# A fused RWKV-6 and max-out MLP kernel: the first units' decay sums in fp32, weight preparation on other engines, and a new order of the list

## The chip, the core and the metric

The kernel runs on one core of a Trainium2 chip. The core has five engines with a queue of instructions each: TensorE (PE, matmuls; its weight loads are shown apart as PEld), VectorE (DVE), ScalarE (ACT), GpSimd (POOL) and SyncE (SP), which here issues all transfers between the chip's memory and the core's. An engine works its queue strictly in order and waits on semaphores where an operand is not there yet. The metric is device microseconds (us) of one execution, the median of several runs. The kernel before takes 164.98 us (five runs, 164.53 to 165.4).

## The reference

Inputs are `r, k, v, w` of 4 sequences x 8 heads x 768 steps x 48, a vector `u` per head, and the weights of a small MLP. The first half is a linear attention with a decay per step and channel; the second a max-out MLP on the 3072 rows that result:

```python
for t in range(S):
    cur = einsum('bhd,bhe->bhde', u[None] * kt, vt)
    y[:, :, t] = einsum('bhd,bhde->bhe', rt, state + cur)
    state = wt[:, :, :, None] * state + einsum('bhd,bhe->bhde', kt, vt)
...
h1 = x @ w1; h2 = x @ w2
g = maximum(h1, h2)
return g @ w_out
```

## The kernel before, in words

**Tiling.** The 768 steps are cut into 6 chunks of 128, and the 4 sequences into 2 pairs. A chunk of one pair is a *unit*; there are 12, numbered 0 to 11, worked in the order chunk 0 pair 0, chunk 0 pair 1, chunk 1 pair 0 and so on. The 128 steps lie on the 128 partitions. Within a unit many steps are made per sequence (`.0` and `.1`).

**The stages of a unit.** `ldw, ldk, ldr, ldv` (L226) load 384 KB each, in pieces of 192 bytes in memory. `lw` (L232, ACT) takes the logarithm of the decay `w`. The running sum of these logarithms over the chunk is a matmul with a triangular matrix, `ex` (L241 to L245). So that it can run on TensorE's reduced fp32 format, the logarithm is split into a high part `lwh` (L236, ACT, a second logarithm written in that format) and a rest `lwl` (L239, DVE), and `ex` is two matmuls that add up in PSUM. From the sum come `incl` (L250, DVE), `aex` and `ainv` (L255, L258, ACT exponentials), and with them the scaled `rp` (L278) and `kp` (L281, both DVE). `T` (L311, PE) transposes these, `TO` (L318, ACT) copies them out of PSUM, `M` (L327, PE) makes the scores, `MO` (L332, DVE) masks them, and `Y` (L343, L347, PE) multiplies by the values `vb` (L304, ACT) and the state. The step's own term is made by `ku` (L288, POOL), `rku` (L292, DVE), `dg` (L297, DVE) and `bv` (L301, POOL), and `YO` (L354, DVE) adds it. `K, sa, sm, sb` carry the state (`sb`, L396, on POOL); `row`, `wt`, `wx` take the chunk's last decay sum through memory (L262, L267) to the layout of the state.

**The MLP.** `X` (L361, PE) and `XO` (L365, ACT) transpose the unit's 256 result rows. The maximum is written as (h1+h2)/2 + |h1-h2|/2. So `H` (L406, PE, four steps a unit, 12 matmuls each group of two) multiplies by the weight difference `wd_sb`, `HO` (L412, ACT) takes half the absolute value, `O1` and `O2` (L416 and L422, PE) multiply by `w_out`, and the linear half goes in one matmul by `wc_sb` = (w1+w2) w_out / 2. `OO` (L431, ACT) copies the result out, `st` (L437, SP) stores it.

**Weight preparation, once.** `ldw12.0` to `.2` load three blocks of w1 and w2 (1 MB each, two transfers), `ldwo.0` and `.1` two halves of `w_out` (768 KB each). These five share two buffers (tag `w12`, L178 and L184), so a block's load waits until the one two places earlier has been used. `wsum` (L196, POOL) and `wdif` (L199, DVE) make sum and difference in bf16; `wT` (L204, PE) transposes the sum into a PSUM tile of tag `mlp`, of which there are two, shared with `H`, `wp`, `O1` and O2; `wTO` (L208, DVE) copies it out; `woc` (L190, POOL) casts `w_out`; `wp` (L213, PE) and `wpO` (L218, ACT) make `wc_sb`. `warm` (L173) are matmuls on a blank tile that keep TensorE busy while there is nothing else.

**What sets the order.** Nothing is scheduled by the compiler. `ORDER` (L17 to L66) is a list written out by hand, one word a step; the steps are issued in that order, each to its engine's queue. So the list fixes the order of every queue, SP's included, and the order in which transfers are asked for. A transfer also waits for the one eight places before it in SP's queue.

Of the kernel before, what the change touches and what calls it, by code (L numbers as in the profile page):

```python
# [26 lines left out]
M.1.0 TO.1.1 H.0.1 MO.1.0 wt.0 ex.3.0 woc.1 HO.0.0 HO.0.1 dg.1.1 H.0.2 ldw.4 incl.3.0 ldv.1.1 M.1.1 HO.0.2
kp.2 wp.0 aex.3.0 rp.2 ex.3.1 row.2 wpO.0 H.0.3 sa.0 bv.1.0 vb.1.0 ldv.2 MO.1.1 aex.3.1 Y.1.0 ldk.3 T.2.0 ku.2
wx.0 HO.0.3 wp.1 TO.2.0 YO.1.0 incl.3.1 lwh.4 wp.2 sm.0 rku.2 lw.4 wpO.1 T.2.1 lwl.4 row.3 vb.1.1 M.2.0 ldw.5
wpO.2 K.1 dg.2 bv.1.1 ldr.3 TO.2.1 Y.1.1 ex.4.0 sb.0.0 O1.0.0 sa.1 vb.2 MO.2.0 sb.0.1 wt.1 aex.4.0 O2.0.0 bv.2  # L30
ainv.3 incl.4.0 K.2 YO.1.1 M.2.1 ex.4.1 sa.2 ku.3 ldr.4 Y.2.0 MO.2.1 aex.4.1 ldk.4 X.1.0 X.1.1 OO.0.0 O1.0.1
XO.1 YO.2.0 lw.5 incl.4.1 O2.0.1 wt.2 kp.3 H.1.0 OO.0.1 lwh.5 X.2.0 rp.3 Y.2.1 H.1.1 HO.1.0 lwl.5 ldw.6 wx.1
T.3.0 HO.1.1 row.4 H.1.2 YO.2.1 TO.3.0 rku.3 H.1.3 ainv.4 ex.5.0 sm.1 X.2.1 ldv.3 HO.1.2 M.3.0 rp.4 T.3.1
ldw.7 XO.2 O1.1.0 MO.3.0 ku.4 HO.1.3 TO.3.1 O2.1.0 ldv.4 dg.3 aex.5.0 H.2.0 OO.1.0 kp.4 M.3.1 wx.2 HO.2.0
H.2.1 incl.5.0 ldk.5 H.2.2 rku.4 HO.2.1 ex.5.1 lw.6 sm.2 O1.1.1 vb.3 sb.1.0 incl.5.1 wt.3 dg.4 HO.2.2 sb.1.1
O2.1.1 lwh.6 bv.3 K.3 MO.3.1 T.4.0 OO.1.1 H.2.3 st.0.0 TO.4.0 lwl.6 st.0.1 O1.2.0 HO.2.3 row.5 sa.3 sb.2.0
vb.4 M.4.0 Y.3.0 sb.2.1 ldr.5 lw.7 MO.4.0 T.4.1 wt.4 bv.4 O2.2.0 aex.5.1 ainv.5 YO.3.0 ex.6.0 K.4 lwh.7
incl.6.0 ku.5 Y.3.1 st.1.0 sa.4 O1.2.1 OO.2.0 ldk.6 YO.3.1 aex.6.0 ldw.8 wx.3 TO.4.1 X.3.0 kp.5 ex.6.1 X.3.1
O2.2.1 XO.3 lwl.7 M.4.1 OO.2.1 st.1.1 Y.4.0 rp.5 aex.6.1 H.3.0 H.3.1 incl.6.1 HO.3.0 sm.3 T.5.0 ainv.6 ldr.6
YO.4.0 H.3.2 HO.3.1 rku.5 ex.7.0 ldv.5 HO.3.2 H.3.3 sb.3.0 MO.4.1 TO.5.0 O1.3.0 ku.6 HO.3.3 dg.5 ldk.7 aex.7.0  # L40
X.4.0 T.5.1 lw.8 incl.7.0 Y.4.1 sb.3.1 TO.5.1 M.5.0 YO.4.1 O2.3.0 MO.5.0 row.6 ex.7.1 OO.3.0 X.4.1 O1.3.1 XO.4
incl.7.1 kp.6 lwh.8 O2.3.1 ldv.6 rp.6 st.2.0 M.5.1 OO.3.1 H.4.0 wx.4 bv.5 MO.5.1 T.6.0 HO.4.0 H.4.1 vb.5 wt.5
H.4.2 lwl.8 aex.7.1 ldw.9 HO.4.1 Y.5.0 ldr.7 K.5 HO.4.2 YO.5.0 ex.8.0 ainv.7 sa.5 H.4.3 rku.6 TO.6.0 Y.5.1
st.2.1 O1.4.0 YO.5.1 vb.6 kp.7 HO.4.3 X.5.0 X.5.1 T.6.1 sm.4 XO.5 wt.6 O2.4.0 dg.6 sb.4.0 aex.8.0 M.6.0 TO.6.1
st.3.0 sb.4.1 H.5.0 incl.8.0 ldw.10 MO.6.0 K.6 bv.6 OO.4.0 ex.8.1 row.7 wx.5 lw.9 H.5.1 incl.8.1 HO.5.0 M.6.1
sm.5 Y.6.0 HO.5.1 rp.7 H.5.2 ainv.8 O1.4.1 sb.5.0 sa.6 lwh.9 row.8 YO.6.0 ku.7 ldv.7 HO.5.2 MO.6.1 T.7.0
st.3.1 X.6.0 O2.4.1 TO.7.0 ldk.8 H.5.3 lwl.9 aex.8.1 ldr.8 T.7.1 OO.4.1 rku.7 lwh.10 Y.6.1 O1.5.0 lw.10 sb.5.1
dg.7 ldk.9 HO.5.3 ex.9.0 YO.6.1 M.7.0 vb.7 bv.7 incl.9.0 O2.5.0 TO.7.1 MO.7.0 O1.5.1 ldv.8 OO.5.0 lwl.10
aex.9.0 X.6.1 O2.5.1 XO.6 ku.8 Y.7.0 OO.5.1 ex.9.1 st.4.0 YO.7.0 wx.6 H.6.0 incl.9.1 H.6.1 HO.6.0 kp.8 M.7.1
HO.6.1 K.7 st.4.1 rp.8 ainv.9 H.6.2 row.9 H.6.3 MO.7.1 aex.9.1 HO.6.2 T.8.0 ldr.9 HO.6.3 st.5.0 O1.6.0 sa.7  # L50
TO.8.0 sm.6 ku.9 ex.10.0 M.8.0 incl.10.0 ldw.11 Y.7.1 T.8.1 aex.10.0 YO.7.1 wt.7 O2.6.0 sb.6.0 vb.8 MO.8.0
X.7.0 sb.6.1 X.7.1 OO.6.0 O1.6.1 XO.7 kp.9 ldv.9 TO.8.1 O2.6.1 rku.8 ldr.10 K.8 OO.6.1 H.7.0 rku.9 H.7.1
HO.7.0 dg.8 st.5.1 M.8.1 HO.7.1 H.7.2 rp.9 ex.10.1 HO.7.2 bv.8 H.7.3 incl.10.1 ldk.10 Y.8.0 MO.8.1 HO.7.3
T.9.0 wt.8 lw.11 O1.7.0 YO.8.0 wx.7 lwh.11 sm.7 Y.8.1 sa.8 TO.9.0 O1.7.1 sb.7.0 ldk.11 YO.8.1 wt.9 sb.7.1 dg.9
ainv.10 X.8.0 X.8.1 O2.7.0 aex.10.1 lwl.11 XO.8 T.9.1 rp.10 ldv.10 M.9.0 OO.7.0 O2.7.1 ldr.11 vb.9 bv.9 MO.9.0
H.8.0 OO.7.1 ex.11.0 HO.8.0 H.8.1 incl.11.0 TO.9.1 st.6.0 Y.9.0 kp.10 H.8.2 aex.11.0 ku.10 YO.9.0 HO.8.1 M.9.1
ex.11.1 HO.8.2 MO.9.1 st.6.1 T.10.0 wx.8 H.8.3 TO.10.0 ldv.11 incl.11.1 K.9 rku.10 O1.8.0 st.7.0 aex.11.1
HO.8.3 sm.8 ainv.11 T.10.1 sa.9 M.10.0 wx.9 TO.10.1 kp.11 Y.9.1 st.7.1 X.9.0 O2.8.0 vb.10 sb.8.0 YO.9.1 O1.8.1
MO.10.0 sb.8.1 X.9.1 rp.11 O2.8.1 XO.9 M.10.1 dg.10 OO.8.0 Y.10.0 OO.8.1 T.11.0 sm.9 H.9.0 TO.11.0 MO.10.1
bv.10 H.9.1 HO.9.0 st.8.0 T.11.1 HO.9.1 st.8.1 H.9.2 sb.9.0 YO.10.0 M.11.0 sb.9.1 HO.9.2 H.9.3 MO.11.0 ku.11  # L60
Y.10.1 HO.9.3 O1.9.0 TO.11.1 YO.10.1 X.10.0 X.10.1 rku.11 O2.9.0 XO.10 O1.9.1 dg.11 OO.9.0 vb.11 M.11.1 bv.11
O2.9.1 MO.11.1 H.10.0 OO.9.1 st.9.0 Y.11.0 HO.10.0 H.10.1 YO.11.0 H.10.2 HO.10.1 st.9.1 Y.11.1 HO.10.2 X.11.0
# [7 lines left out]
def kernel(  # L70
# [19 lines left out]
    FO = d_ff // C  # L90
# [17 lines left out]
    triU = const.tile([C, C], F32)  # L108
    make_upper_triangular(nc, triU, val=1.0, diag=False)
    triR = const.tile([C, C], F32R)  # L110
# [8 lines left out]
    for i in range(2):  # L119
        eng = nc.vector if i == 0 else nc.gpsimd  # L120
        rp = const.tile([C, NB, H, DP], BF16, name=f"rp{i}")
        kp = const.tile([C, NB, H, DP], BF16, name=f"kp{i}")
# [18 lines left out]
    ws_sb = const.tile([C, KO, d_ff], BF16)  # L141
    wo_sb = const.tile([C, FO, HD], BF16)
    wsT_sb = const.tile([C, FO, HD], BF16)
# [3 lines left out]
    st = {}  # L147
# [4 lines left out]
    def flat(x):  # L152
        return x.rearrange("p h d -> p (h d)")
# [14 lines left out]
    def warm(tag):  # L168

        def fn(count):  # L170
            x = ps.tile([C, 512], F32, tag=tag, bufs=2 if tag == "mlp" else 1, name="warm")
            for _ in range(count):
                nc.tensor.matmul(x, ident, blank)  # L173
        return fn
# [12 lines left out]
        st["wof", half] = x  # L187

    def woc(half):
        nc.gpsimd.tensor_copy(wo_sb[:, half * FO // 2:(half + 1) * FO // 2, :], st["wof", half])  # L190

    def ldu():
        nc.sync.dma_start(out=u_b, in_=u.rearrange("h d -> (h d)").unsqueeze(0).to_broadcast([C, HD]))

    def wsum(ko):
        nc.gpsimd.tensor_add(ws_sb[:, ko, :], st["w12", ko][:, 0, :], st["w12", ko][:, 1, :])  # L196

    def wdif(ko):
        nc.vector.tensor_sub(wd_sb[:, ko, :], st["w12", ko][:, 0, :], st["w12", ko][:, 1, :])  # L199
# [5 lines left out]
        st["wT", ko] = tp  # L205

    def wTO(ko):
        nc.vector.tensor_copy(wsT_sb[:, :, ko * C:(ko + 1) * C], st.pop(("wT", ko)))  # L208

    def wp(ko):  # L210
        wc_p = ps.tile([C, HD], F32, tag="mlp", bufs=2)
# [28 lines left out]

    def ex(i, b):  # L241
        ex_p = ps.tile([C, HD], F32, tag="ex", name="ex_p")
        nc.tensor.matmul(ex_p, triR, flat(st["lwh", i][:, b]), start=True, stop=False)  # L243
        nc.tensor.matmul(ex_p, triR, flat(st["lwl", i][:, b]), start=False, stop=True)  # L244
        st["ex", i, b] = ex_p  # L245

    def incl(i, b):
# [186 lines left out]
    def out_st(i, b):  # L434
# [5 lines left out]
               ldw=ld("w", w), ldk=ld("k", k), ldr=ld("r", r), ldv=ld("v", v),  # L440
               lw=lw, lwh=lwh, lwl=lwl, ex=ex, incl=incl, aex=aex, ainv=ainv, row=row, wt=wt, wx=wx, rp=rp, kp=kp,
               ku=ku, rku=rku, dg=dg, bv=bv, vb=vb, T=T, TO=TO, M=M, MO=MO, Y=Y, YO=YO, X=X, XO=XO,
               K=K, sa=sa, sm=sm, sb=sb, H=Hf, HO=HO, O1=O1, O2=O2, OO=OO, st=out_st, **{f"warm_{t}": warm(t) for t in ('kv',)})
    with tc.manual_schedule():
        for step in ORDER.split():
            name, *at = step.split(".")
# [38 lines left out]
```

## Time and profile before

| | us |
|---|---|
| median of 5 runs (lowest, highest) | 164.98 (164.53, 165.4) |
| the profiled execution, whole | 164.53 |
| its span in the profile | 162.8 |
| busy: PE, DVE, ACT, POOL | 148.8, 133.7, 118.4, 75.9 |
| of PE's, the warm matmuls (68 recorded) | 19.1 |
| first matmul of `H.0.0`; of `O1.0.0` | 33.58; 47.42 |
| DVE's last instruction ends | 148.9 |
| PE's last matmul ends; last `OO` starts | 159.4; 159.50 |

The page of a profile cuts the span in 40 slices and gives each engine's busy share in tenths. The windows view gives the busy time in chosen stretches. The timeline lists instructions with start and length, and, in brackets, how long the engine had stood idle and what released it. The groups view sums instructions of one line. Lengths overlap a little: consecutive DVE instructions listed with 0.55 us start 0.47 apart.

### The profile page before, as it was taken

To read this page: it belongs to the slowest core of one execution; us is meant where nothing else is said; L and a number is where in the kernel's file an instruction comes from. 1 tells how busy PE (TensorE), PEld (TensorE's weight loads), DVE (VectorE), ACT (ScalarE), POOL (GpSimd) and SP (SyncE) were. 2 spreads that over 40 slices of the span, in tenths; PEclk is the share of its full clock that TensorE was granted. 3 is DMA by queue.
4 is the path that set the end of the run, shared out by engine and by line. 5 is a ranking of instruction groups with operands and counts; after the bars stand their busy time and mean duration, and the time that the engine had idled before them with its cause. 6 is when DMAs were issued, how large, how long until landed. Compare 5 with 4: busy or idle time off the path is not lost.

```text
span 162.8 us, 3999 instructions
## 1 busy us (share of the span) xinstructions
PE 148.8 (91%) x1604; PEld 101.9 (63%) x1606; DVE 133.7 (82%) x171; ACT 118.4 (73%) x202; POOL 75.9 (47%) x68
## 2 busy tenths in 40 slices
PE   6997798659979999999899999999999999999991
PEld 2444444447656865768668678677777677767760
DVE  3296999899979999999998999999989999762000
ACT  5153743775797997898969998987789796765641
POOL 8284597451685085832530375932158343730000
PEclk9999999999999999999999999999999999999999
DMA  5989998998999899599999829978899932011202
GB/s 101 322 171 259 377 220 174 268 299 139 207 227 155 153 229 224 131 197 212 234 187 207 187 59 261 212 209 164 189 171 206 229 109 76 25 52 48 79 17 97
DMA packets 112758, 28.82 MB, mean 177 GB/s; under 512 B 107738, under 2 KB 111962, under 8 KB 112740
## 3 DMA queue, kind: packets, MB, share of 16 engines
q1 hardware_dynamic: 112740, 28.58, 80.7%
q8 instruction: 12, 0.20, 0.5%
q14 instruction: 6, 0.05, 0.1%
HBM read 23.82 MB, written 4.75 MB: 176 GB/s over the span
## 4 chain that ended last, share of the span: by engine, by line
PE 48%; DVE 22%; SPq 12%; DMA 7%; issue 6%; ACT 3%; DVEq 0%; ACTq 0%
PE o_p L416 15%; PE g_p L406 12%; SPq L226 9%; PE o_p L422 6%; DVE MTm L332 5%; DMA rt<-in_r_dram 3%; PE tp L311 3%; DMA wt<-in_w_dram 3%; PE mt_p L327 3%; PE y_p L343 3%; DVE ku L292 3%; DVE dg L297 2%; DVE xs L354 2%; PE ex_p L243 2%; DVE rp L278 2%
## 5 line engine op out<-in xcount | busy, mean ns | idle before, releaser
L406 PE MATMUL g_p<-xT,wd_sb 128*128 128x256 bf16 x288 | 37.8, 273 | 2.0 <-ACT xT L365 1.4
L416 PE MATMUL o_p<-wo_sb,gT 128*128 128x384 bf16 x192 | 37.5, 326 | 0.0
L412 ACT ACTIVATE gT<-g_p 128x512 bf16<-128x512 f32 x48 | 28.2, 599 | 8.0 <-PE g_p L406 7.4
L301 POOL TENSOR_TENSOR bv<-vt,dg 128x768 f32<-128x768 f32 (+1 forms) x14 | 21.0, 1500 | 22.1 <-issue 8.1
L406 PEld LDWEIGHTS <-wd_sb 128*128 128x128 bf16 x288 | 26.3, 98 | 7.7 <-issue 3.2
L332 DVE TENSOR_TENSOR MTm<-mt_p,triU 128x1024 bf16<-128x1024 f32 x24 | 29.1, 1211 | 2.1 <-PE mt_p L327 2.1
L288 POOL TENSOR_TENSOR ku<-kt,u_b 128x768 f32<-128x768 f32 (+1 forms) x14 | 24.6, 1758 | 9.4 <-DMA kt<-in_k_dram 7.6
L318 ACT COPY rkT<-tp 128x1024 bf16<-128x1024 bf16 x24 | 24.4, 1017 | 5.0 <-PE tp L311 5.0
L396 POOL CAST sz<-sf 48x384 bf16<-48x384 f32 x20 | 14.1, 703 | 27.7 <-DVE sf L389 17.5
L416 PEld LDWEIGHTS <-gT 128*128 128x128 bf16 x192 | 18.0, 98 | 11.0
L173 PE MATMUL warm<-blank,ident 128*128 128x512 bf16 x68 | 19.1, 425 | 1.6 <-POOL ident masks.py:199 1.5
L255 ACT ACTIVATE Aex<-ex_p 128x384 f32<-128x384 f32 x24 | 11.9, 497 | 10.3 <-PE ex_p L244 6.5
L239 DVE TENSOR_TENSOR lwl<-lw,lwh 128x768 fp32r<-128x768 f32 (+1 forms) x14 | 15.9, 1144 | 3.2 <-ACT lwh L236 2.0
L292 DVE TENSOR_TENSOR ku<-rt,ku 128x768 f32<-128x768 f32 (+1 forms) x14 | 16.7, 1195 | 1.2 <-POOL ku L288 1.2
L431 ACT COPY osb<-o_p 128x384 f32<-128x384 f32 x24 | 11.6, 487 | 7.2 <-PE o_p L416 6.3
L278 DVE TENSOR_TENSOR rp<-rt,Aex 128x768 bf16<-128x768 f32 (+1 forms) x14 | 14.6, 1039 | 2.3 <-ACT Aex L255 2.3
L354 DVE TENSOR_TENSOR xs<-y_p,bv 128x384 bf16<-128x384 f32 x24 | 13.2, 548 | 3.1 <-PE y_p L347 2.4
L422 PE MATMUL o_p<-wc_sb,xT 128*128 128x384 bf16 x72 | 15.7, 326 | 0.0
L250 DVE TENSOR_TENSOR incl<-ex_p,lw 128x384 f32<-128x384 f32 x24 | 13.1, 548 | 1.2 <-PE ex_p L244 0.9
L232 ACT ACTIVATE lw<-wt 128x768 f32<-128x768 f32 (+1 forms) x14 | 10.5, 753 | 4.6 <-DMA wt<-in_w_dram 3.2
L173 PEld LDWEIGHTS <-ident 128*128 128x128 bf16 x70 | 6.9, 107 | 9.8 <-issue 3.2
L281 DVE TENSOR_TENSOR kp<-kt,Ainv 128x768 bf16<-128x768 f32 (+1 forms) x14 | 12.3, 881 | 0.1
(54 smaller groups left out, 231.4 us busy)
## 6 DMA issues: line engine op xcount, KB each, us to landing
out_dram<-osb SPq DMA_DIRECT2D x24, 192.0 KB, 2.0
wt<-in_w_dram SPq DMA_DIRECT2D x10, 384.0 KB, 4.4
kt<-in_k_dram SPq DMA_DIRECT2D x10, 384.0 KB, 5.7
rt<-in_r_dram SPq DMA_DIRECT2D x10, 384.0 KB, 7.3
vt<-in_v_dram SPq DMA_DIRECT2D x10, 384.0 KB, 4.3
w<-in_moe_w_dram SPq DMA_DIRECT2D x6, 512.0 KB, 5.4
wof<-in_moe_w_out_dram SPq DMA_DIRECT2D x2, 768.0 KB
wt<-in_w_dram SPq DMA_DIRECT2D x4, 192.0 KB, 5.7
```

Of the source, the lines that this page charges most:

```text
L173: nc.tensor.matmul(x, ident, blank)
L278: nc.vector.tensor_mul(rps[i % 2][:, seqs(b), :, 0:D], get("r", i, b), get("Aex", i, b))
L288: nc.gpsimd.tensor_mul(rows_(x), rows_(get("k", i, b)), u_b.unsqueeze(1).to_broadcast([C, x.shape[1], HD]))
L292: nc.vector.tensor_mul(rows_(get("ku", i, b)), rows_(get("r", i, b)), rows_(get("ku", i, b)))
L301: nc.gpsimd.tensor_mul(x, get("v", i, b), get("dg", i, b).unsqueeze(3).to_broadcast(list(x.shape)))
L318: nc.scalar.copy(rkT, st.pop(("tp", i, b)))
L332: nc.vector.tensor_mul(x.rearrange("p a q c -> p (a q) c"), st.pop(("mt", i, b)).rearrange("p a q c -> p (a q) c"), triU.unsqueeze(1).to_b ...
L354: nc.vector.tensor_add(x, st.pop(("y", i, b)), flat(st["bv", i][:, b]))
L406: nc.tensor.matmul(g_p[:, q, :], wd_sb[:, ko, fo * C:(fo + 1) * C], st["xT", i][:, ko].rearrange("p b c -> p (b c)"), start=(ko == 0), sto ...
L412: nc.scalar.activation(st["gT", i][:, f2 * 2:f2 * 2 + 2, :], st.pop(("g", i, f2)), AF.Abs, scale=0.5)
L416: nc.tensor.matmul(st["o", i, b], st["gT", i][:, fo, b * C:(b + 1) * C], wo_sb[:, fo, :], start=False, stop=(fo == FO - 1))
L422: nc.tensor.matmul(st["o", i, b], st["xT", i][:, ko, b, :], wc_sb[:, ko, :], start=(ko == 0), stop=False)
```

## The change

It has five parts.

1. `ex` looks whether the unit has a low part. If not, it is one matmul in full fp32 of the logarithm itself with the fp32 triangle. Units 0, 1 and 2 have no `lwh` and `lwl` any more (five of each in the list: two halves of unit 0, two of unit 1, unit 2 whole). The other units are as before.
2. `wsum` moves from POOL to DVE.
3. `wTO` moves from DVE to ACT.
4. `woc` moves from POOL to ACT.
5. The list is reordered from its first word to its last. It holds 57 warm matmuls where it held 70, some of them in other PSUM tiles (`warm_mt`, `warm_y`). Loads: k0.0 is second where r0.0 was; the second weight block comes after unit 0's loads and half of unit 1's; the third block comes after unit 0's values, unit 2's decay and the first half of `w_out`, where it had been before all of these.

```diff
 ORDER (beginning; loads up to the third weight block)
-ldw.0.0 ldr.0.0 ldw12.0 ldw.0.1 lw.0.0 ldk.0.0 lwh.0.0 lwl.0.0 ldw.1.0 warm_kv.10 ex.0.0 aex.0.0 ldw.1.1
-rp.0.0 ldu wdif.0 ldk.0.1 lw.0.1 incl.0.0 wsum.0 ldr.0.1 lwh.0.1 ainv.0.0 ldw12.1 lw.1.0 lwh.1.0 lwl.0.1
-ldw12.2 lwl.1.0 warm_kv.22 ex.0.1 ku.0.0 wT.0 incl.0.1 ku.0.1 aex.0.1 ldv.0.0 ainv.0.1 warm_kv.3 ex.1.0 lw.1.1
+ldw.0.0 ldk.0.0 ldw12.0 ldu lw.0.0 ldw.0.1 warm_kv.8 ex.0.0 ldr.0.0 incl.0.0 ldk.0.1 ldr.0.1 ldw.1.0 ku.0.0
+ldr.1.0 wsum.0 lw.0.1 ainv.0.0 aex.0.0 ldw12.1 kp.0.0 warm_kv.13 ex.0.1 rp.0.0 ldk.1.0 wT.0 incl.0.1 T.0.0
+wdif.0 ainv.0.1 aex.0.1 wTO.0 ku.0.1 ldw.1.1 TO.0.0 rku.0.0 ldv.0.0 lw.1.0 warm_kv.12 ex.1.0 ldv.0.1 incl.1.0
+ldw.2 rku.0.1 aex.1.0 wdif.1 ldwo.0 wsum.1 lw.1.1 ainv.1.0 rp.0.1 row.0 warm_kv.14 wT.1 kp.0.1 M.0.0 rp.1.0
+ex.1.1 kp.1.0 T.0.1 ldw12.2 aex.1.1 MO.0.0 TO.0.1 ldw.3 incl.1.1 lw.2 warm_kv.4 M.0.1 dg.0.0 T.1.0 vb.0.0
+dg.0.1 bv.0.0 ex.2.0 vb.0.1 MO.0.1 TO.1.0 bv.0.1 Y.0.0 YO.0.0 woc.0 ku.1.0 warm_kv.3 Y.0.1 X.0.0 YO.0.1
+aex.2.0 ldwo.1 ainv.1.1 warm_mt.2 X.0.1 incl.2.0 ldk.1.1 XO.0 wsum.2 warm_y.1 ex.2.1 ldr.1.1 wTO.1 K.0 wdif.2
...
     def woc(half):
-        nc.gpsimd.tensor_copy(wo_sb[:, half * FO // 2:(half + 1) * FO // 2, :], st["wof", half])
+        nc.scalar.copy(wo_sb[:, half * FO // 2:(half + 1) * FO // 2, :], st["wof", half])
...
     def wsum(ko):
-        nc.gpsimd.tensor_add(ws_sb[:, ko, :], st["w12", ko][:, 0, :], st["w12", ko][:, 1, :])
+        nc.vector.tensor_add(ws_sb[:, ko, :], st["w12", ko][:, 0, :], st["w12", ko][:, 1, :])
...
     def wTO(ko):
-        nc.vector.tensor_copy(wsT_sb[:, :, ko * C:(ko + 1) * C], st.pop(("wT", ko)))
+        copy = (nc.scalar.copy, nc.scalar.copy, nc.scalar.copy)[ko]
+        copy(wsT_sb[:, :, ko * C:(ko + 1) * C], st.pop(("wT", ko)))
...
     def ex(i, b):
         ex_p = ps.tile([C, HD], F32, tag="ex", name="ex_p")
-        nc.tensor.matmul(ex_p, triR, flat(st["lwh", i][:, b]), start=True, stop=False)
-        nc.tensor.matmul(ex_p, triR, flat(st["lwl", i][:, b]), start=False, stop=True)
+        if ("lwl", i) in st:
+            nc.tensor.matmul(ex_p, triR, flat(st["lwh", i][:, b]), start=True, stop=False)
+            nc.tensor.matmul(ex_p, triR, flat(st["lwl", i][:, b]), start=False, stop=True)
+        else:
+            nc.tensor.matmul(ex_p, triU, flat(st["lw", i][:, b]))
         st["ex", i, b] = ex_p
```

In the new list the steps that follow the part shown are, per engine, up to the first `O1`: PE `wT.2 M.1.0 H.0.0 H.0.1 ex.3.0 H.0.2 T.1.1 wp.1 wp.0 M.1.1 Y.1.0 wp.2 ex.3.1 K.1 H.0.3 Y.1.1 O1.0.0`; DVE `sa.0 incl.2.1 rku.1.0 lwl.3 dg.1.0 kp.1.1 rp.1.1 MO.1.0 sm.0 rku.1.1 dg.1.1 incl.3.0 MO.1.1 YO.1.0 kp.2 incl.3.1 sa.1 YO.1.1 rp.2 rku.2 lwl.4 dg.2 MO.2.0`; ACT `aex.2.1 lw.3 lwh.3 wTO.2 HO.0.0 woc.1 HO.0.1 HO.0.2 wx.0 TO.1.1 ainv.2 wpO.1 vb.1.0 aex.3.0 vb.1.1 wpO.0 wpO.2`.

## The prediction

> **What bounds the kernel.** I read the page's slices first, then the stages, then single lines of the timeline. The page:
>
> ```profile
> span 162.8 us, 3999 instructions
> PE 148.8 (91%) x1604; PEld 101.9 (63%) x1606; DVE 133.7 (82%) x171; ACT 118.4 (73%) x202; POOL 75.9 (47%) x68
> ...
> PE   6997798659979999999899999999999999999991
> ...
> DVE  3296999899979999999998999999989999762000
> ...
> DMA  5989998998999899599999829978899932011202
> ```
>
> Three rows stand at nine together: PE from slice 12, DVE from slice 4 to 33, the transfers up to slice 32. The stages (start:end, length, then busy us of PE, PEld, DVE, ACT, POOL) say the same in us:
>
> ```profile
> 20.00:30.00 10.00, 8.41 (x53) 4.11 (x55) 9.79 (x14) 4.22 (x8) 7.74 (x5) 1.00 1.04 199
> 30.00:40.00 10.00, 7.35 (x101) 5.62 (x99) 9.46 (x14) 7.72 (x14) 4.01 (x3) 1.00 1.00 256
> 40.00:50.00 10.00, 8.78 (x117) 5.95 (x115) 8.95 (x13) 8.41 (x15) 7.43 (x7) 1.00 1.07 201
> 50.00:60.00 10.00, 10.00 (x116) 7.76 (x113) 9.92 (x13) 9.09 (x16) 4.06 (x3) 1.00 0.94 171
> ...
> 130.00:150.00 20.00, 20.00 (x250) 14.86 (x249) 14.65 (x20) 14.68 (x24) 7.63 (x7) 1.00 0.19 66
> ```
>
> From 50 on PE is busy almost without a gap, and DVE nearly so until 130. What PE does before 30 is mostly warm matmuls: they fill 8.10, 5.38 and 5.63 us of the first three tens. So the time is "when does real work on PE and DVE get going" plus a fixed rest. Only the first 50 us can give much; after that an order can only add gaps. Between 130 and 150 DVE has 5 us to spare, and loads come early by then (w.11 is asked for at 108.8, used at 119.7), so in the end PE counts.
>
> **Transfers set the start.** They are served in the order asked for, at a price that I read from what starts the moment its data lands:
>
> ```profile
> 8.55 3.40 POOL L196 TENSOR_TENSOR ws_sb<-w 128x1024 bf16<-128x1024 f32 x1 [3.46 <-DMA w<-in_moe_w_dram]
> ...
> 10.11 2.72 DVE L239 TENSOR_TENSOR lwl<-lw,lwh 128x384 fp32r<-128x384 f32 x2
> ...
> 18.14 2.37 POOL L196 TENSOR_TENSOR ws_sb<-w 128x1024 bf16<-128x1024 f32 x1 [2.57 <-DMA w<-in_moe_w_dram]
> ...
> 20.88 3.41 POOL L196 TENSOR_TENSOR ws_sb<-w 128x1024 bf16<-128x1024 f32 x1 [0.38 <-DMA w<-in_moe_w_dram]
> ...
> 26.97 1.23 POOL L288 TENSOR_TENSOR ku<-kt,u_b 128x384 f32<-128x384 f32 x1 [0.91 <-DMA kt<-in_k_dram]
> ...
> 30.09 1.00 POOL L288 TENSOR_TENSOR ku<-kt,u_b 128x384 f32<-128x384 f32 x1 [0.78 <-DMA kt<-in_k_dram]
> ...
> 33.70 1.54 POOL L190 CAST wo_sb<-wof 128x1536 bf16<-128x1536 f32 x1 [2.62 <-DMA wof<-in_moe_w_out_dram]
> ...
> 35.85 1.47 POOL L190 CAST wo_sb<-wof 128x1536 bf16<-128x1536 f32 x1 [0.61 <-DMA wof<-in_moe_w_out_dram]
> ```
>
> Read the starts. Block 2 to block 3 of the weights: 20.88 - 18.14 = 2.74 us a block. k1.0 to k1.1, with whole w3 between: 3.12 us for three half loads, 1.04 each (2.08 a whole one). wof0 to wof1: 2.15. Now the new order, from the first block (8.5 as before: as many bytes stand ahead): u 9.3; w0.1 10.1; five halves (r0.0, k0.1, r0.1, w1.0, r1.0) 15.3; block 2 18.0; k1.0, w1.1, v0.0, v0.1 22.2; w2 24.3; wof0 26.6; **block 3 29.4** (before 20.9); w3 31.4; wof1 33.6 (before 35.85); k1.1 and r1.1 35.7 (before some 31); k2 37.8; v1.0 38.8, v1.1 39.9 (before 40.7 and 45.0, where `bv` waits for them); r2 42.0. By 35.7 both orders have brought the same data; what differs is who waits meanwhile. SP itself is held only where wof1 waits for `woc.0` (28.3 below); 5 us of transfers are queued then, so nothing runs dry.
>
> **The parts on their engines.** DVE loses five `lwl`, which took 0.56 + 2.72 (two) + 0.94 + 1.58 = 5.8 us, and three `wTO`, 2.0; it gains three `wsum`, for which the nearest row is `wdif`, 1.17 from start to start: 3.5. Net -4.3. ACT loses five `lwh` (4 x 0.51 + 0.84 = 2.9), gains three `wTO` (nearest row: `TO`, same shape, 0.9 start to start: 2.7) and two `woc` (by the casts of `vb`, 0.50 at 384 columns and 0.84 at 768, so 0.34 more per 384: 1.5 each): net +2.8, late, between 26 and 42. POOL loses 9.2 + 3.0. The 2.72 above is part of why: the two half `lwl`, otherwise 0.47 apart, ran beside POOL's 3.40 us `wsum`. "SBUF — State Buffer" of the Trainium skill, section "SBUF: two separate sides", states that a DVE instruction with two SBUF inputs and a GpSimd one reading SBUF lock each other out. That speaks against part 2, for `wsum` on DVE has two such inputs as well; by it, each that meets a `ku` would cost up to 1 us more, but POOL's `ku` are over at 13 and 27, and `wsum` runs at 8.5, 19 and 29.4.
>
> fp32 `ex`: no row shows one. Lower bound 0.33 us (one pass like L244's), a gain of 0.13 on the 0.46 between the starts of an `ex` and the next step; upper, four times L243's 0.466: 1.9, or 1.4 more each. I take 0.7, close to the pair's 0.70 in the chain. The first five lie beside warm matmuls or DVE work that is not late. At the upper end `ex.1.1` and `ex.2.0` push `MO.0.1` and `YO.0.0` by about 1 us, which the wait for block 3 swallows; without that cover it would be 1 us of the end. "FP8 and Floating Point Precision", section "TensorE Precision Notes", speaks of four passes for true fp32; if each pass cost L244's 0.33, the six would take 1.3 each, 3.6 us more in all than I take, most of it behind the same cover.
>
> The 13 warm matmuls fewer (0.25 each when going well) cost nothing by themselves. The first ten ran at 0.445, the next 22 at 0.245, though the granted clock reads 1.00 for both; a PE that stands still might fall back to the first figure. Gaps up to 1.36 us did not do that here. I see at most 2 us in the new order; if it happens, the price is about 1.5.
>
> **Laying out the start.** DVE, start to start: 0.47 a half step, 0.87 a whole one, 1.13 `MO`, 1.17 weights. Block 2 at 18.0, so `wdif.1`, `wsum.1` 20.3; `rp.0.1 kp.0.1 rp.1.0 kp.1.0` 22.2; `MO.0.0` 23.3, `incl.1.1`, two `dg` 24.8, `MO.0.1` 26.0, both `YO.0` 26.9, `incl.2.0` 27.4. Then DVE waits for block 3: `wsum.2`, `wdif.2` 29.4 to 31.7, and `H.0.0` starts near 31.8 (before 33.58). `sa.0 incl.2.1 rku.1.0 lwl.3 dg.1.0` to 34.3, `kp.1.1`, `rp.1.1` as they land, 36.2; `T.1.1` 36.6.
> ACT: `TO.1.0` 26.9, `woc.0` 28.3, `aex.2.0 ainv.1.1 XO.0` 29.8, `wTO.1` 30.7, `aex.2.1 lw.3 lwh.3` 32.9, `wTO.2` 33.8, `HO.0.0` 34.3, `woc.1` 35.8, `HO.0.1`, `HO.0.2` 36.8, `TO.1.1` 37.9, `ainv.2 wpO.1 vb.1.0` 39.4.
> PE: `wp.1` (1.3) after `T.1.1`, 37.9; `wp.0` 39.2; `M.1.1 Y.1.0` 39.9; `wp.2` 41.2; `ex.3.1 K.1 H.0.3 Y.1.1` (0.46, 0.37, 0.66, 0.38) 43.1. There `O1.0.0` starts, before at 47.42. But the old list had by then also done `T.2.0, T.2.1, M.2.0, ex.4.0` (0.45, 0.45, 0.33, 0.46 = 1.7), so PE's lead is 47.42 - 43.1 - 1.7 = **2.6 us**. DVE: `MO.1.1` waits for `M.1.1` (39.5) and ends at 40.6, and `YO.1.0 kp.2 incl.3.1 sa.1 YO.1.1 rp.2 rku.2 lwl.4 dg.2` bring `MO.2.0` to 47.0, before 47.94, with one `YO` (0.47) more behind it: lead **1.4 us**.
>
> **Sum.** With both engines near full to 130, the smaller lead is what lasts: -1.4. The profiled execution's own 164.53 (span 162.8 and 1.7 around it) becomes 163.1; it lies 0.45 under the median shown, so against the median 164.98 - 1.4 = **163.6**. The rest of the list is shuffled too; the counts per engine do not change there, and the old one left PE only some 2 us of gaps from 50 to 150, so I count it at nothing, with +-2 for the range.
>
> **Rivals.** (a) *Slower: block 3 becomes the wait.* Its load is moved back by 8.5 us, and `wsum.2`, `wdif.2` stand in DVE's queue ahead of all of unit 1's second half; DVE was 98% busy at 20 to 30 before, and now stands from 27.4. Every us that block 3 lands later costs DVE one. At 30.8 the 1.4 is used up. The mean rate of the page's third row, 177 GB/s, where blocks now reach the page's 377, would bring it near 32; gaps of 1 to 2 us in the shuffled middle then come on top: 165.5 to 167.3. For it: slices at 139 to 174 GB/s. Against: the prices above reproduce every landing before. Chance 0.32.
> (b) *No change: ACT takes the lead back.* ACT is full from 26 to 42 in my layout, with 5.7 us of new work there; `wTO.2` and `woc.1` hold the two `mlp` tiles and so `H.0.1` and `wp.1`. One more us there and the middle's gaps give 164.5 to 165.5. For it: ACT was 72 to 84% busy at 30 to 50 already; against: `lwh` is gone, and PE has 1.2 us more lead than I count. Chance 0.16.
> (c) *Faster by the whole of PE's lead:* if DVE's 5 spare us at the end make up its part, 164.98 - 2.6 = 162.4, with bare luck in the middle 161.0. Chance 0.17; my forecast, 162.9 to 164.4, has 0.35.
> (d) *fp32 is not used* where a low part exists; the new list issues none before `lwl.3`, so all six are fp32: as good as excluded.
>
> The chances: faster by over 0.3% (about 0.5 us, what a measurement of this kernel can tell from no change) 0.35 + 0.17 = 0.52, within 0.16, slower 0.32. The range takes in (a)'s far end, because it holds a third: 161.0 to 167.3.
>
> **What would show it.** Right: `wsum.2` starts on DVE within 1 us of 29.4 after an idle; first `g_p` near 32; first `o_p` near 43; PE again at 9.8 or more of each ten from 50 on; DVE's last step near 147.5. Wrong: `wsum.2` past 31, six fp32 `ex` well over 1 us each, half `ws_sb` steps of 2 us and more beside POOL, or PE gaps of several us between 50 and 130 that wait for DVE or ACT.

## The result and the profile after

The changed kernel takes 166.63 us (median of 43 runs, 164.71 to 170.5); the kernel before 164.87 (80 runs, 163.16 to 168.18). The ratio is **1.0096, 95% interval 1.0078 to 1.0115: slower by 1.0%**. The forecast was 1.4 us faster: the sign is wrong, and the time lies within the range that was given. Some executions of every kernel are slower, often at a lowered granted clock; all ratios, and the medians given for the experiments below, are of the undisturbed ones (for the changed kernel 28 runs, median 166.27).

The profiled execution took 164.97 us (span 163.2), near the fast end of the kernel's runs. Its page has these counterparts of the lines shown before:

```profile
span 163.2 us, 3952 instructions
PE 148.2 (91%) x1591; PEld 101.4 (62%) x1593; DVE 129.6 (79%) x166; ACT 120.9 (74%) x202; POOL 64.0 (39%) x63
...
PE   6949988769999989998999899869998999999991
...
DVE  3163797998999999999997999999999995873000
...
DMA  5999999898999997998998989627999902011202
```

The engines moved as the change says: DVE has 4.1 us less than before, ACT 2.5 more, POOL 11.9 less. But PE's row, nearly all nines from slice 12 on before, now has dents in the middle. Taken as one stage, 50 to 130 us (busy us of PE, PEld, DVE, ACT, POOL in that order), first before, then after:

```profile
50.00:130.00 80.00, 78.27 (x945) 57.69 (x942) 78.25 (x96) 69.43 (x120) 37.31 (x29) 1.00 0.97 190
```

```profile
50.00:130.00 80.00, 75.53 (x932) 55.22 (x931) 78.08 (x95) 67.35 (x114) 39.86 (x30) 1.00 0.94 190
```

PE idles 4.5 us there, 1.7 before; DVE has 98% in both; the granted clock reads 1.00 in both.

**The start did what it should.** Two lines each of DVE's and of PE's timeline of after (start, duration):

```profile
28.85 1.22 DVE L195 TENSOR_TENSOR ws_sb<-w 128x1024 bf16<-128x1024 f32 x1
...
47.35 1.23 DVE L335 TENSOR_TENSOR MTm<-mt_p,triU 128x1024 bf16<-128x1024 f32 x1 [0.24 <-PE mt_p L330]
```

```profile
31.05 0.83 PE L409 MATMUL g_p<-xT,wd_sb 128*128 128x256 bf16 x6
...
42.40 0.65 PE L425 MATMUL o_p<-wc_sb,xT 128*128 128x384 bf16 x3
```

`wsum.2` starts at 28.85 and waits for no load, the first `H` at 31.05 (before 33.58), the first `O1` at 42.40 (before 47.42). With the 1.7 us of other PE work that the old list had done by then, PE is 3.3 us ahead.

**It is lost in the middle.** The largest loss, at unit 8, on DVE, POOL and PE:

```profile
102.61 0.94 DVE L239 TENSOR_TENSOR lwl<-lw,lwh 128x768 fp32r<-128x768 f32 x1
103.48 3.02 DVE L281 TENSOR_TENSOR rp<-rt,Aex 128x768 bf16<-128x768 f32 x1
106.43 1.25 DVE L284 TENSOR_TENSOR kp<-kt,Ainv 128x768 bf16<-128x768 f32 x1
```

```profile
102.83 1.09 POOL L399 CAST sz<-sf 48x384 bf16<-48x384 f32 x1 [0.55 <-DVE sf L392]
103.89 1.80 POOL L291 TENSOR_TENSOR ku<-kt,u_b 128x768 f32<-128x768 f32 x1
105.75 1.12 POOL L399 CAST sz<-sf 48x384 bf16<-48x384 f32 x1
```

```profile
106.56 0.40 PE L314 MATMUL tp<-ident,rp 128*128 128x128 bf16 x4 [1.18 <-DVE rp L281]
107.74 0.40 PE L314 MATMUL tp<-ident,kp 128*128 128x128 bf16 x4 [0.78 <-DVE kp L284]
```

An undisturbed `rp` takes 0.95. This one is issued while POOL works on `sz`, POOL's `ku.9` follows at once, and `rp.8` ends 0.8 us after `ku.9` does: it has waited for both. PE, whose next step is the transposes of `rp`, stands 1.18 us and then 0.78. Behind smaller collisions of this kind (`rp` 2.23, `lwl` 2.34 and 2.37) PE stands 0.64, 0.69 and 0.48 us, and once 0.42. All these waits end with DVE, none directly with ACT or a load. (Behind the 0.69 the `lwl` of 2.34 had first waited 0.93 for ACT's `lwh`; in `e7` below it waits 0.92 as well, and PE has no gap.)

### The profile page after: what moved, and what is told of

Its sections match the earlier page's. It is cut to its first block, busy times and chain, and to the rows that moved or that the text cites. A ratio compares the mean times of both kernels' runs of the same rounds, so it can differ in the third digit from the quotient of the medians.

```text
span 163.2 us, 3952 instructions
## 1 busy us (share of the span) xinstructions
PE 148.2 (91%) x1591; PEld 101.4 (62%) x1593; DVE 129.6 (79%) x166; ACT 120.9 (74%) x202; POOL 64.0 (39%) x63
## 4 chain that ended last, share of the span: by engine, by line
PE 54%; DVE 23%; DMA 9%; ACT 6%; issue 4%; SPq 2%; DVEq 0%; ACTq 0%
PE o_p L419 13%; PE g_p L409 13%; DMA wt<-in_w_dram 6%; PE o_p L425 5%; DVE MTm L335 5%; PE tp L314 4%; DVE rp L281 4%; DMA rt<-in_r_dram 3%; DVE ku L295 3%; PE mt_p L330 3%; PE wc_p L213 2%; DVE kp L284 2%; PE y_p L346 2%; PE warm L172 2%; DVE incl L253 2%
## 5 line engine op out<-in xcount | busy, mean ns | idle before, releaser
L409 PE MATMUL g_p<-xT,wd_sb 128*128 128x256 bf16 x288 | 37.1, 273 | 1.3 <-ACT wsT_sb L208 1.3
L419 PE MATMUL o_p<-wo_sb,gT 128*128 128x384 bf16 x192 | 37.0, 326 | 0.0
L304 POOL TENSOR_TENSOR bv<-vt,dg 128x768 f32<-128x768 f32 (+1 forms) x14 | 20.2, 1449 | 38.4 <-DVE dg L300 19.6
L399 POOL CAST sz<-sf 48x384 bf16<-48x384 f32 x20 | 14.9, 747 | 27.8 <-DVE sf L392 17.1
L172 PE MATMUL warm<-blank,ident 128*128 128x512 bf16 x55 | 16.3, 439 | 1.6 <-POOL ident masks.py:199 1.5
L258 ACT ACTIVATE Aex<-ex_p 128x384 f32<-128x384 f32 x24 | 11.9, 495 | 6.9 <-DVE incl L253 3.5
L281 DVE TENSOR_TENSOR rp<-rt,Aex 128x768 bf16<-128x768 f32 (+1 forms) x14 | 15.8, 1127 | 0.3 <-DMA rt<-in_r_dram 0.3
L261 ACT ACTIVATE Ainv<-incl 128x768 f32<-128x768 f32 (+1 forms) x14 | 10.5, 752 | 4.6 <-DVE incl L253 4.6
L295 DVE TENSOR_TENSOR ku<-rt,ku 128x768 f32<-128x768 f32 (+1 forms) x14 | 13.3, 953 | 0.0
L239 DVE TENSOR_TENSOR lwl<-lw,lwh 128x768 fp32r<-128x768 f32 x9 | 11.3, 1258 | 0.9 <-ACT lwh L236 0.9
```

The source lines that it names most:

```text
L281: nc.vector.tensor_mul(rps[i % 2][:, seqs(b), :, 0:D], get("r", i, b), get("Aex", i, b))
L295: nc.vector.tensor_mul(rows_(get("ku", i, b)), rows_(get("r", i, b)), rows_(get("ku", i, b)))
L304: nc.gpsimd.tensor_mul(x, get("v", i, b), get("dg", i, b).unsqueeze(3).to_broadcast(list(x.shape)))
L409: nc.tensor.matmul(g_p[:, q, :], wd_sb[:, ko, fo * C:(fo + 1) * C], st["xT", i][:, ko].rearrange("p b c -> p (b c)"), start=(ko == 0), sto ...
L419: nc.tensor.matmul(st["o", i, b], st["gT", i][:, fo, b * C:(b + 1) * C], wo_sb[:, fo, :], start=False, stop=(fo == FO - 1))
```

## The experiments

Names of steps are those of the list. The line numbers in an experiment's profile differ by a few from those of after, since its list fills other lines.

**First group: which part of the list?** Theory M: the lead is given back in PE's waits for DVE. C: a lowered clock after PE's gaps. E: the moved work itself costs more.

`e1` takes the list of after up to `MO.2.0` and then the steps of before's list that are left; `e2` the reverse, with before's engines. The cut below is where `e1` leaves after's list.

```diff
 OO.0.0 dg.2 XO.1 M.2.0 row.3 T.2.1 OO.0.1 MO.2.0
-H.1.0 TO.2.1 ex.4.0 rp.3 H.1.1 HO.1.0 wt.1 aex.4.0
...
+TO.2.1 ex.4.0 vb.2 wt.1 aex.4.0 bv.2 incl.4.0 K.2
...
```

> The new kernel's list up to MO.2.0 (about 48 us), then the old list's order for all steps still to do; all five parts of the change are in. Theory M (the new start brings its lead, the new order of the middle gives it back in PE gaps that wait for VectorE): the old middle keeps the lead of about 3 us, 161.5 to 163.5. Theory C (the gaps and fewer warm matmuls of the new start lower TensorE's granted clock, and that is the loss): as slow as the new kernel, 166 to 167. Theory E (the moved work on ScalarE and VectorE costs more than I took): 165.5 to 167.

165.79 us, ratio to before 1.0109 (1.0029 to 1.019). M misses by 2 us or more, and the time lies in E's range. The large gaps are gone, but a new one of 1.75 us stands at the seam: `K.2` waits for `vb.2` and that for a load. The granted clock behind it is 0.50 at 52 to 54 us, so this run does not decide.

> The old kernel and its list up to MO.2.0, then the new order for the steps still to do. Theory M: no lead to begin with and the new middle, so slower than either, 167 to 169. Theory C: the old start keeps the clock, 164.5 to 165.5. Theory E: nothing moved, 164.5 to 165.5.

168.06 us (two runs, 167.4 and 168.71), ratio 1.0232 (1.0081 to 1.0384), as M has it. The gaps of after's middle stand here too (0.64, 0.69, 1.19, 0.78, 0.48), at the same steps: they belong to the middle of the list, not to the new start.

`e3` is the code of after with the list of before, less its ten `lwh` and `lwl` of units 0 to 2; `e4` the code of before with the list of after, with these ten put in behind `lw`.

```diff
 # e3: old list
-        nc.gpsimd.tensor_add(ws_sb[:, ko, :], st["w12", ko][:, 0, :], st["w12", ko][:, 1, :])
+        nc.vector.tensor_add(ws_sb[:, ko, :], st["w12", ko][:, 0, :], st["w12", ko][:, 1, :])
...
```

> The old list unchanged but for the ten words lwh and lwl of units 0 to 2, with fp32 decay sums there, wsum on VectorE, wTO and woc on ScalarE: parts 1 to 4 without part 5. Theory M: VectorE has 4 us less to do in a start that it bounds, so 162.5 to 164.5. Theory C: the old warm matmuls stand, so as theory M or the old time, 163 to 165. Theory E: 165.5 to 167.

166.79 us, ratio 1.0143 (1.0047 to 1.024): again in E's range and not in M's. PE waits for ACT between 30 and 40, 1.36 us for `xT` as before, and 2.81 for `gT`, which stands behind the `wTO` and the two `woc` that ACT has been given. The middle's gaps are before's small ones.

> The new list with the old split sums in units 0 to 2 (their lwh and lwl put right behind lw) and the old engines for wsum, wTO and woc: part 5 without parts 1 to 4. Theory M: the new middle and a slower start, 167 to 169. Theory C: the new warm matmuls, so 166 to 167 or a little more. Theory E: without the moved work 164 to 165.5.

172.04 us (three runs), ratio 1.0481 (1.0344 to 1.0619), where E said 164 to 165.5 and M 167 to 169. So neither half works alone; with the new list the fp32 sums and the moved work are worth about 6 us, and E falls.

**Second group: one step, and POOL's share.**

```diff
 # e5 and e12
-lwh.10 T.8.1 MO.8.0 ku.9 ldr.9 O1.6.0 HO.6.3 row.8 TO.8.1 YO.7.1 O2.6.0 dg.8 sb.6.1 vb.8 M.8.1
+lwh.10 T.8.1 MO.8.0 ldr.9 O1.6.0 HO.6.3 row.8 TO.8.1 YO.7.1 O2.6.0 dg.8 sb.6.1 vb.8 ku.9 M.8.1
```

> The kernel after with one word of its list moved: ku.9, GpSimd's product of k and u for unit 9, stands behind vb.8 instead of ahead of sb.6.1. Theory M (the new middle loses the lead where VectorE operations are stretched beside GpSimd's) says the two PE gaps of unit 8 (1.18 and 0.78 us) shrink to under 0.5 together, rp.8 takes under 1.5 us instead of 3.02, and the time falls by 1.5 to 2 us below the kernel after: about 164.7. A rival, that VectorE's whole work is what runs late there, says that the gap only moves on to the next unit and the time falls by less than 0.5 us.

> The kernel after with ku.9 alone moved, once more, for a profile (the first one fell in an execution in which PE ran at half speed throughout). Theory M says that rp.8 takes under 1.5 us, the gaps of 1.18 and 0.78 us are gone, the other gaps (0.64, 0.69, 0.48) stand, and the time is about 164.4.

164.36 us (11 runs, ratio to before 0.9987, 0.9948 to 1.0025) and again 164.75 (12 runs, 0.9975, 0.9936 to 1.0014). One step of the list, moved, takes back 1.8 to 2.0 us of after by these ratios and after's 1.0096, and 2.8 by `e6` on the same chip. DVE and POOL at that place in `e12`:

```profile
104.80 1.25 DVE L278 TENSOR_TENSOR rp<-rt,Aex 128x768 bf16<-128x768 f32 x1
105.98 1.25 DVE L281 TENSOR_TENSOR kp<-kt,Ainv 128x768 bf16<-128x768 f32 x1
```

```profile
104.14 2.28 POOL L396 CAST sz<-sf 48x384 bf16<-48x384 f32 x2 [0.55 <-DVE sf L389]
106.51 2.41 POOL L288 TENSOR_TENSOR ku<-kt,u_b 128x768 f32<-128x768 f32 x1
```

`rp.8` takes 1.25 between the two `sz`, and `ku.9` comes after it; the two gaps of PE shrink from 1.96 to 0.36 us. Theory M has this right in place and, with 1.5 to 2 us expected, about right in size. The other gaps do not all stand as expected: one is 1.16 instead of 0.64, one 0.28 instead of 0.42.

`e6` is after, unchanged.

> The kernel after once more, unchanged, on the same chip as the others here: its median by earlier runs is 166.6 us. Theory M says that the gaps of PE in the middle (0.64, 0.69, 1.18, 0.78, 0.48) stand again at the same instructions, since they follow from the list and the stretched VectorE operations. Theory C (a lowered clock after PE gaps makes the loss) says that the clock is under 0.95 in some slices right after the start's 2.2 us gap or the 2 us gap of unit 8, and that the time goes with the mean clock.

167.17 us, ratio 1.017 (1.0117 to 1.0222). In its profiled execution (166.38 us, span 164.6) the granted clock is 1.00 in every stage up to 160 us, and its other runs with clocks of 0.996 to 1.0 took 166.36 to 167.19. **Theory C falls**: at full clock the kernel is as slow. This execution also shows one way in which after's runs come to lie above its first profile. `rp.5` in `e6`, with POOL beside it:

```profile
69.53 2.69 DVE L281 TENSOR_TENSOR rp<-rt,Aex 128x768 bf16<-128x768 f32 x1
```

```profile
68.88 1.09 POOL L399 CAST sz<-sf 48x384 bf16<-48x384 f32 x1 [3.21 <-DVE sf L392]
69.94 1.47 POOL L304 TENSOR_TENSOR bv<-vt,dg 128x768 f32<-128x768 f32 x1
```

and the same three in the first profile of after:

```profile
69.15 1.25 DVE L281 TENSOR_TENSOR rp<-rt,Aex 128x768 bf16<-128x768 f32 x1
```

```profile
68.49 1.10 POOL L399 CAST sz<-sf 48x384 bf16<-48x384 f32 x1 [3.21 <-DVE sf L392]
69.86 1.88 POOL L304 TENSOR_TENSOR bv<-vt,dg 128x768 f32<-128x768 f32 x1 [0.27 <-DMA vt<-in_v_dram]
```

There `bv` had to wait 0.27 us for its load, and in that pause DVE got in; in `e6` POOL went on without a pause and DVE waited 1.4 us more. A quarter of a microsecond of a transfer goes with 1.4 us of DVE here.

`e7` and `e8` leave POOL's `ku` and `bv` out from unit 2 on, of after and of before.

```diff
     def ku(i, b=None):
         x = new("ku", i, b)
+        if i >= 2:
+            return
         nc.gpsimd.tensor_mul(rows_(x), rows_(get("k", i, b)),
...
-        nc.vector.tensor_add(x, st.pop(("y", i, b)), flat(st["bv", i][:, b]))
+        nc.vector.tensor_add(x, st.pop(("y", i, b)), flat(st["bv" if i < 2 else "v", i][:, b]))
```

> The kernel after with GpSimd's ku and bv left out from unit 2 on (the own-step term then lacks u and its row sums' product with v; v itself is added). GpSimd then has little left that reads beside VectorE. Theory M says that VectorE's rp, kp, rku and lwl go back to about 0.95 us, the middle gaps of PE sum to under 1.5 us instead of 4.2, and this kernel is as fast as or faster than the next one, which leaves the same out of the kernel before: 161 to 163 us. Theory E (the copies and casts moved to ScalarE and the sums to VectorE cost more by themselves) says that it stays 1 to 2 us slower than the next one.

> The kernel before with the same GpSimd work left out from unit 2 on. Theory M says it gains less than the kernel after gains from it, since its middle gaps of PE sum to 1.7 us only: 162.5 to 164 us. Theory E says that both gain alike, about 1 us, and the one made from the kernel after stays 1 to 2 us behind.

160.34 us (six runs, ratio to before 0.9755, 0.9705 to 0.9804) and 162.09 (three runs, 0.9867, 0.9799 to 0.9936). The stage 50 to 130 of `e7`, then of `e8`:

```profile
50.00:130.00 80.00, 80.00 (x1000) 59.71 (x999) 76.40 (x103) 72.30 (x124) 12.30 (x16) 1.00 0.96 197
```

```profile
50.00:130.00 80.00, 80.00 (x996) 59.75 (x994) 73.54 (x99) 72.51 (x125) 9.90 (x16) 1.00 0.94 195
```

PE has no gap any more, in either. DVE of `e7`, which does the same steps as in after, is busy 8.0 us less in the whole span (121.6 against 129.6): that was waiting beside POOL, counted as busy. `e7` is now 1.8 us *faster* than `e8`: by the ratios after gains 3.4% by what is left out, before 1.3%. PE's lead in this pair, by the first `O1` (42.53 against 46.80) and the 1.7 us of other work, is 2.6 us; most of it shows in the time once DVE no longer holds PE up.

**Third group: the new start with the old middle, mended.**

```diff
 # e9, against e1: after's list kept through Y.2.0
 M.2.0 row.3 T.2.1 OO.0.1 MO.2.0
+H.1.0 TO.2.1 ex.4.0 rp.3 H.1.1 HO.1.0
...
+H.1.3 HO.1.2 MO.2.1 K.2 Y.2.0
...
 # e10, against e1: one load moved
-HO.0.3 O1.0.0 sa.1 ldr.3 sb.0.1 ainv.3 YO.1.1 ldv.2 rp.2
+HO.0.3 O1.0.0 sa.1 ldv.2 ldr.3 sb.0.1 ainv.3 YO.1.1 rp.2
```

> New start and old middle once more, but the list of after is kept some 7 us longer, through Y.2.0, before the list of before takes over, so that K.2 is no longer asked for before v of unit 2 has landed. Theory M says that the 1.75 us gap of the seam goes, the middle keeps the small gaps of before (1.7 us in all), and the lead of the start (3.3 us by the first o_p) is seen in the time: 161.5 to 163 us. A rival, that the rest of the time is set by the transfers or by VectorE's whole work whatever the start, says that the time stays within 1 us of before: 164 to 165.5.

> The first kernel with the new start and the old middle, with one word moved: the load of v for unit 2 is issued ahead of the load of r for unit 3, so it should land about 2 us earlier. Theory M says that the gap of 1.75 us before K.2 falls under 0.3 and the time to 162 to 163.5; the rival says that another load, now later by 2 us, makes a gap of the same size elsewhere and the time stays at 164.5 to 166.

165.14 us (1.0025, 0.9989 to 1.0062) and 165.73 (1.004, 1.0001 to 1.0079). **Here M misses by 2 us or more and its rival's time is right.** In `e9` the seam's gap is gone, but smaller ones come in its place (0.36, 0.52, 0.55, 0.61: two for DVE's `xs`, one for DVE's `lwl`, one for ACT's `lwh`); in `e10` `K.2` still waits 1.43, and behind that wait the granted clock is 0.50 at 52 to 54 us, which this run does not separate from the rest. So neither shows PE's lead in the time. The reading from here on, called V: DVE's steps, together with their waits beside POOL, set the pace from 45 us on, PE runs into DVE, and a lead of PE alone is worth little.

```diff
 # e11, against e5: four DVE steps put behind one that PE waits for; the first
-lwl.5 XO.2 O2.1.1 OO.1.0 rp.4 M.3.0 st.0.0 OO.1.1 ex.5.0 ldk.5 ainv.4 bv.3 MO.3.0 H.2.0
+lwl.5 XO.2 O2.1.1 OO.1.0 M.3.0 st.0.0 OO.1.1 ex.5.0 ldk.5 ainv.4 bv.3 MO.3.0 rp.4 H.2.0
...
 # e16, against e11: two loads exchanged
-OO.1.1 ex.5.0 ldk.5 ainv.4
+OO.1.1 ex.5.0 ldr.5 ainv.4
...
-lwh.6 ldr.5 Y.3.0
+lwh.6 ldk.5 Y.3.0
```

> The kernel after with five words moved: ku.9 behind vb.8 as before, and on VectorE rp.4 behind MO.3.0, rp.5 behind MO.4.0, lwl.8 behind MO.6.0, lwl.11 behind incl.10.1, so that the operations that PE waits for do not stand behind one that GpSimd's transfer-free products hold up. Theory M says that the gaps of PE in the middle sum to under 1.5 us and the time falls to 162 to 163.5. If VectorE's total of work or the transfers bind there, the gaps come back behind later operations and the time stays at about 164.4, as with ku.9 alone.

> The kernel after with the five moves and a sixth: the load of k for unit 5 changes places with that of r for unit 5, so that GpSimd's ku.5 starts some 2 us later, beside MO.3.1 and YO.3.0, and not over kp.4, which took 2.11 us there. Theory V says that the gaps left in unit 3 and 4 (1.03 and 1.20 us) fall under 0.8 together and the time to 162 to 163. If the transfers bind there, r of unit 5 or k of unit 5 is late for rp.5 or kp.5 and the time stays at 163.9 or grows.

`e11`: 163.23 us (three runs, 0.9844, 0.9753 to 0.9935); PE's gaps in the middle were 2.4 us by its profile (an execution of 164.11 us), not under 1.5, since `kp.4` now met `ku.5`. `e16`: **163.17 us, ratio 0.9922 (0.9889 to 0.9955): faster than both kernels**, though just short of the 162 to 163 expected. `kp.4` is back to 0.94 and the two gaps of 1.03 and 1.20 are one of 0.72, as expected; but `kp.5` now met a `bv`, PE stood 1.44 us there, and the gaps sum to 2.6. In its stage

```profile
50.00:130.00 80.00, 77.15 (x957) 57.16 (x952) 77.87 (x97) 69.27 (x119) 40.30 (x30) 1.00 0.95 193
```

DVE is as full as ever and PE still idles 2.9 us: there is more to be had by such moves.

**Fourth: DVE relieved with nothing left out.** All decay sums in fp32, from after (`e13`) and from before (`e14`); `lwh` and `lwl` are gone.

```diff
 # e13: every lwh and lwl taken from the list
-H.0.0 lwh.3 incl.2.1 ldv.1.0 rku.1.0 wTO.2 lwl.3 HO.0.0
+H.0.0 incl.2.1 ldv.1.0 rku.1.0 wTO.2 HO.0.0
...
```

> The kernel after with fp32 decay sums in all units: its nine whole lwl and nine lwh are gone. VectorE does 7.8 us less (nine of 0.87) and is no longer beside GpSimd in them; PE does more, 18 times about 0.28 us (an fp32 ex holds PE 0.70 to 0.75 from its start to the next step, the pair 0.45), 5.0 us. Theory V, into which M has turned (VectorE's work and its waits beside GpSimd set the end from 45 us on, and the last VectorE step is followed by a fixed 13.9 us of PE) says that the gaps of PE that wait for VectorE fall from 4.2 us to under 1, that PE sets the end now, and that the time is about after's less 4 and plus 5: 165 to 167. The rival, that something else in the list makes the gaps, says that they stay and the 5.0 us come on top: 170 to 172.

> The kernel before with fp32 decay sums in all units, no lwl and lwh. Theory V says that PE sets the end here as well, with 1.7 us of gaps to save and 5.0 us of PE work more after the start: 167 to 169, that is 2 to 3 us behind the run made from the kernel after in the same way, as with GpSimd's work left out; the lead of the new start then stands in the time. The rival says the two differ by after less before, the kernel from after staying 1 to 2 us slower.

`e13`: 164.80 us (1.0011, 0.9982 to 1.0039), `e14` 165.01 (1.0049, 1.0012 to 1.0086). The stage of `e13`:

```profile
50.00:130.00 80.00, 79.81 (x947) 57.27 (x946) 69.76 (x90) 65.03 (x110) 39.59 (x30) 1.00 0.98 197
```

PE's waits for DVE in the middle are gone though POOL does all it did: a second proof, with another cure, that DVE made them (not that POOL did, for DVE has less work here and PE more). An fp32 `ex` holds PE 0.65 to 0.75 us, the pair about 0.45, and PE sets the end, just under V's figure. `e14` misses V's by 2 to 4 us: it is level with `e13` instead of behind. It has lost the five early `lwl` too, so it holds part of the change's own start (`MO.2.0` at 47.35 by its profile, as in after); whether that is the whole reason stays open.

## Why the forecast was wrong, step by step

- *Landing times and layout: right.* `wsum.2` 28.85 (29.4 was laid out; by the prediction's own prices `wof0` lands at 26.4 and not 26.6, and block 3 at 29.2), first `H` 31.05 (31.8), first `O1` 42.40 (43.1), `MO.2.0` 47.35 (47.0). Rival (a) gave the sign and a range that holds the time, but its main mechanism did not happen, since block 3 had landed when DVE came to it; the gaps in the shuffled middle, which it put on top, did.
- *fp32 `ex` at 0.7 us: right.* It shows as two matmul records of 0.49 to 0.59 and holds PE 0.64 to 0.75 us, once 0.84. The four passes for true fp32 of "FP8 and Floating Point Precision" of the Trainium skill (section "TensorE Precision Notes"), by the prediction's estimate of 0.33 us each, would have made 1.3; this trace does not bear that price out.
- *DVE -4.3, ACT +2.8, POOL -12.2: right* (-4.1, +2.5, -11.9). But DVE's 4.2 us less of busy time between 0 and 50 became idle time there (40.8 of 50 us busy before, 36.6 after), since DVE waits for loads and ACT in the start.
- *PE's lead 2.6, DVE's 1.4:* measured 3.3, and 0.6 (47.94 less 47.35) plus one `YO` (0.47), so about 1.1.
- *"PE that stands still ... the price is about 1.5":* the 2.21 us gap before `ex.0.1` came with a granted clock of 0.50 and 0.72 in the next 4 us, and 11 warm matmuls took 3.85 us. In `e6` the clock was not lowered there and the first `H` came at 31.21, no earlier than after's 31.05. The price was nothing there, since mostly warm matmuls were slowed.
- **The step that failed: "The rest of the list is shuffled too ... I count it at nothing", and with it "the smaller lead is what lasts".** From `MO.2.0` to DVE's last step before took 100.9 us (47.94 to 148.9), after 102.0 (47.35 to 149.3) and in `e6` 103.2 (47.52 to 150.7). DVE's lead of 1.1 turned into a lag of 0.4 to 1.8. `MO.2.0` and the last step of before, then the last step of after:

```profile
47.94 1.21 DVE L332 TENSOR_TENSOR MTm<-mt_p,triU 128x1024 bf16<-128x1024 f32 x1
...
148.32 0.56 DVE L354 TENSOR_TENSOR xs<-y_p,bv 128x384 bf16<-128x384 f32 x1 [1.05 <-PE y_p L347]
```

```profile
148.76 0.56 DVE L357 TENSOR_TENSOR xs<-y_p,bv 128x384 bf16<-128x384 f32 x1 [1.05 <-PE y_p L350]
```

- The end of the span comes 13.9 us after DVE's last step in all these profiles but `e7`'s (14.4). That alone does not show that DVE sets the end: this last step waits 1.05 us for PE. The gaps show it: PE, 3.3 us ahead at the first `O1`, ends its last matmul 0.4 behind (159.9 against 159.4). Of these 3.7 us, 2.7 are gaps (4.47 us from 50 to 130, against 1.73); the last 1.0 went into PE steps that stand a little further apart than before, which no run explains.
- What made the gaps is named by the runs: DVE steps with two SBUF inputs waiting beside POOL. Summing, from 50 us on, what each DVE step takes above the median of its own kind in the same profile: 8.5 us before, 9.8 after, 10.1 in `e6`, 8.7 in `e12`, 7.5 in `e16`, 1.3 in `e7`. So most of the waiting was already in the kernel before; the new list adds some 1.5 us and places it where PE has nothing queued. PE gaps of several us between 50 and 130 that wait for DVE are what the prediction named as a sign that it is wrong.
- The prediction had the rule in hand ("SBUF — State Buffer" of the Trainium skill, section "SBUF: two separate sides", says that one of the two engines then blocks for the other's whole instruction; `rp.8` behind `ku.9` agrees) and applied it to three `wsum` only. DVE's 98% from 50 to 130, which it called "near full", held some 8 us of waiting: that row was the place to look.
- Rival (b): ACT took nothing back; no gap of PE in the middle ends with ACT. The wait for `wTO.2` that it names is there (`H.0.1` stands 1.25 us for it), but it ended at 33.1, not after the 33.8 laid out. (ACT was 77 and 84% busy at 30 to 50 before, not 72 to 84.)

The cause of the sign is settled by `e5`/`e12` and `e7`/`e8`, with `e13` for DVE's part. How much of PE's lead can be had with the whole computation stays open: 1.8 us between `e7` and `e8`, 0.2 between `e14` and `e13`.

## What to carry to other kernels

Where two engines are near full, a busy share may hold waiting: compare each step's duration with the shortest of its shape, and look at what the other engine does beside it, before calling a reordered stretch neutral. A lead won by one of two coupled engines may not last where the other does not have it too (`e9` and `e10` point that way). Where DVE and POOL collide, move the POOL step (or the load that releases it) beside DVE steps that read PSUM; one such step was worth about 2 us here.

## What the runs showed of the hardware

- A DVE step with two SBUF inputs that meets a POOL step waits for it, and is mostly let in when that step ends, even if POOL's next one follows at once. `rp.3` of after ends 0.82 us after `bv`, though the records of `bv` and `ku` overlap by 0.03 us, and it is `ku` that is drawn out:

```profile
57.17 2.23 DVE L281 TENSOR_TENSOR rp<-rt,Aex 128x768 bf16<-128x768 f32 x1
```

```profile
56.52 2.06 POOL L304 TENSOR_TENSOR bv<-vt,dg 128x768 f32<-128x768 f32 x1 [0.54 <-POOL sz L399]
58.55 2.52 POOL L291 TENSOR_TENSOR ku<-kt,u_b 128x768 f32<-128x768 f32 x1
```

- It was passed over where the step that ended was an `sz` and a `ku` or `bv` followed at once (records overlapping by 0.03 or 0.04 us): `rp.8` (3.02 us instead of 0.95), `rp.5` in `e6` (2.69), and one `rku` of the kernel before (2.84, at 76.49). With a pause of 0.06 behind `sz` (`e12`) or 0.27 (after's `rp.5`) it got in. Why `sz` differs is not shown. `MTm` (one input in PSUM) kept its 1.21 us beside `bv` and `ku`.
- The granted clock fell after some gaps of PE of 1.4 us and more (0.50 at 12 to 14 us in after's profile, behind 2.21; 0.50 at 52 to 54 in `e10`, behind 1.43), and not after others (1.93 us in `e6`, 2.08 in `e13`, clock 1.00).
- In one execution of `e5` PE ran at half speed from start to end (365.42 us; the 288 `g_p` matmuls 534 ns each instead of 273), with a granted clock that reads 1.0. It came once, and its cause is not known.
